# Attention feeding a soft mixture of experts: spread weight loads as halves, move some transposes and the logits in the order of work

## The chip, the cores and the metric

One Trainium2 chip, one of its cores. The metric is the device time of one execution in microseconds (us), the median over several runs. The engines go by these names: PE or TensorE (matrix products and transposes), DVE or VectorE, ACT or ScalarE, POOL or GpSimd, and SP or SyncE, which here only issues transfers (DMAs). A name with q (SPq) is an engine's instruction queue. PSUM is the memory that TensorE writes to.

## The reference, cut to what matters

```python
# 1. attention: 4 batches, 8 heads, 512 local and 32 global positions, head size 64
out_l = softmax(q_l @ [k_g, k_l masked to a window of 32 each side]) @ [v_g, v_l]
out_g = softmax(q_g @ [k_g, k_l]) @ [v_g, v_l]
x = concat(out_g, out_l)                 # as 2176 rows of 512
# 2. soft mixture of experts: 8 experts, 4 slots each
logits = x @ phi                         # phi: 512 x 32
slot_input = softmax(logits over rows).T @ x
slot_out[e] = relu(slot_input[e] @ w1[e]) @ w2[e]   # w1: 512 x 1024, w2: 1024 x 512
x = softmax(logits over slots) @ slot_out
# 3. two dense layers with a squared relu
h = x @ w_in;  out = (relu(h) ** 2) @ w_out
```

## The kernel before

The work has three stages. The attention stage takes the heads in groups of four: eight groups g, two to a batch, and each group in four tiles of 128 rows, so 32 steps n = 4g + uu. The expert stage multiplies the 32 slot inputs with the experts' weights, 32 blocks of 1 MB. The last stage does the two dense layers.

In the attention stage a step has three parts, on different engines. `emit_S` (L357): scores on TensorE (L369) into two PSUM buffers of the pool "S", their minimum on VectorE (L376, the sign is turned), the exponential on ScalarE (L380). `emit_T` (L383): four transposes of the probabilities (L388) into a buffer "T", copied out by ScalarE (L163, the line of the helper `copy_on`). `emit_PV` (L392): products with v (L400), then the division on VectorE (L407 to L409) into `xb`, the tile's output. For each group there are also the global rows: `glob_S` (scores L423 into a buffer "S" and the single buffer "M", minimum L428 to L430, exponentials L434 and L438), `glob_T` and `glob_PV` (L459, copied to `x_g` by four small copies, L471). The pools: "S" has three buffers, "T" three, "M" one, and the products with v one, "X".

When both groups of a batch are through, its four output tiles are transposed (`x_T`, L478: transposes L481, then a copy by ScalarE). Tiles 0 and 3 use a buffer "S" for that, tiles 1 and 2 a buffer "T". `logits` (L486) multiplies the transposed tiles with phi (L493, into "M" in the first three batches), takes the maximum on VectorE (L499), the exponential on ScalarE (L506), and updates running sums (L521, L525). `slot_E` and `slots` (L534, L542) follow. The last batch's work is cut up differently, at the stage's end, but its tiles 0 and 1 go by the same places.

Loads: q and k of two heads come by `load_qk` (L232) on SP into one pair of buffers, and VectorE sorts them (`sort_qk`, L242) before they are transposed (L310, L327); so the next load waits for the sort. v comes by `load_v` (L247): the global part on SP, the local part on POOL from group 2 on. POOL also makes shifted copies of v (`prep_win`, L340), which wait until the products with the old copies are done; VectorE makes others (L350, L352). The expert blocks come on SP into a ring of 13 buffers "w", then into buffers that the attention stage gives up: `more_weights` (L133) issues the next block, `release(n)` raises the limit by n and issues them.

The order of the work is written out by hand: all five engines keep program order (`manual_schedule` with 'PADSG'). `at(when, fn, ...)` gives each piece a place counted in steps, and the pieces are issued in the order of their places. `POS` (L50) holds the places of what occurs once a group, relative to 4g; `LASTPOS` (L51) has other places for the last groups (for group 6 the global scores, transposes and products). The pieces around the change, for a batch whose second group is g, counted from 4g: products of tile 1 at 1.6, x0 at 1.756, global scores at 1.806, scores of the next group's tile 0 at 2.1, transposes of tile 3's probabilities at 2.2, x1 at 2.555; products of tile 2 at 2.6 and tile 3 at 3.6, global products at 3.655, x2 at 3.8, scores at 4.1, x3 at 4.158; scores at 5.1, transposes of probabilities at 5.2, the next q at 5.3, the logits at 5.351, the next k at 5.4. `WAT` (L62) lists the 13 steps at which an expert block is issued, `RELEASE` (L53) the places of the further ones.

Of the kernel before, what the change touches and what calls it, by code (L numbers as in the profile page):

```python
# [9 lines left out]
F32 = mybir.dt.float32  # L10
# [36 lines left out]
MAN = 'PAD'  # L47
MANA = 'PADSG'
ESORT = [0, 0]
POS = {'load0': -7.545, 'sort0': -5.099, 'sort1': -3.55, 'glob_S': 1.806, 'glob_T': 2.7, 'glob_PV': 3.655, 'w1': -2.548, 'w4': -0.34, 'w7': -0.339, 'w10': -1.245, 'w13': 1.7, 'v0': -1.648, 'v1': 0.25, 'x0': 1.756, 'x1': 2.555, 'x2': 3.8, 'x3': 4.158, 'L': 5.351, 'E': 5.8, 'sl': 6.752, 'qg': 1.158}  # L50
LASTPOS = {('glob_S', 6): 0.55, ('glob_T', 6): 1.75, ('glob_PV', 6): 3.35, ('glob_S', 7): -0.3, ('glob_T', 7): 0.35, ('glob_PV', 7): 1.7, ('v0', 7): 0.05, ('v1', 7): 2.05, ('w1', 1): -0.75, ('v0', 0): -0.75, ('sort0', 1): -5.95}  # L51
QGF = 0
RELEASE = ((25.85, 3), (27.75, 1), (29.15, 1), (30.85, 2))  # L53
# [5 lines left out]
EX = 'act'  # L59
EE = 'act'  # L60
EW = 'act'
WAT = [2, 3, 5, 7, 9, 10, 13, 14, 15, 15, 18, 19, 19]  # L62
RECTS = 'A0-1 B0-2 C0-4 A2-6 B3-8 C5-10 A7-12 B9-15 A13-15 C11-15'
RING = 13
MORE = 5
# [8 lines left out]
def kernel(  # L74
# [7 lines left out]
    nc = tc.nc  # L82
    const = ctx.enter_context(tc.tile_pool(name="const", bufs=1))
    ring = ctx.enter_context(tc.tile_pool(name="ring", bufs=RING, side="right"))
# [19 lines left out]
    specs = []  # L104
    for kind, q in UNITS:
        es = slice(2 * q, 2 * q + 2)
        for m in range(4):
            src = (
                w1[es, m * 128:(m + 1) * 128, :].rearrange("e p f -> p e f") if kind == "w1" else
                w2[es, m * 256:(m + 1) * 256, :].rearrange("e (p t) d -> p e (t d)", t=2)  # L110
            )
# [4 lines left out]
    wt, raw = {}, {}  # L116
    w_in32, w_out32 = w_in.bitcast(I32), w_out.bitcast(I32)
    st = {"next": 0, "limit": RING}

    def slot(tag, shape, dt, nm):  # L120
        return ring.tile(shape, dt, tag=tag, name=nm, bufs={"w": RING, "k": MORE, "m": LAST}[tag])

    def load_raw(f, tag="k", halves=(0, 1)):
        if 0 in halves:
            raw[f] = slot(tag, [128, 2048], I32, "raw")
            nc.sync.dma_start(
                out=raw[f][:, 0:1024].rearrange("p (k w) -> p k w", k=4),
                in_=w_in32[:, 256 * f:256 * f + 256].rearrange("(k p) w -> p k w", p=128),
            )
        if 1 in halves:  # L130
            nc.sync.dma_start(out=raw[f][:, 1024:2048], in_=w_out32[128 * f:128 * f + 128, :])

    def more_weights(n=1):  # L133
        for _ in range(n):
            i = st["next"]
            if i >= len(specs) or i >= st["limit"]:
                return
            key, src = specs[i]
            if i == ALL:

                wt[key] = bp.tile([128, NT * 128], F32, tag="cT", name="extra")[:, 0:2048].rearrange(
                    "p (e f) -> p e f", e=2
                )
                nc.sync.dma_start(out=wt[key], in_=src)
                st["next"] += 1
                continue
            j = (i - (i > ALL)) % ALL
            if key[0] == "raw":
                load_raw(0, "w", [key[1]])
                st["next"] += 1  # L150
                continue
            t = slot("w" if j < RING else "k" if j < RING + MORE else "m", list(src.shape), F32, f"ring{i}")
            nc.sync.dma_start(out=t, in_=src)
            wt[key] = t
            st["next"] += 1

    def release(n):
        st["limit"] += n
        more_weights(n)
# [518 lines left out]
    def at(when, fn, *args):  # L678
        order.append((when, len(order), fn, args))
# [7 lines left out]
    for g in range(NG):  # L687
        b, gq = g // 2, g % 2
        a = lambda name: 4 * g + (LASTPOS.get((name, g)) or POS[name])
        for p in range(2):  # L690
# [28 lines left out]
    at(-0.98, load_phi)  # L719
    at(POS["qg"], prep_global_q)  # L720
    at(2.19, slot_sums)
    at(steps - 2 + 0.8, lambda: x_T(B - 1, "g", x_g))
    at(steps - 1 + 0.5, last_xT, B - 1)
    for when in WAT:
        at(when + 0.9, more_weights)
    for when, n in RELEASE:
        at(when, release, n)
    for when, n in BUSYS:
# [8 lines left out]
    x3 = xb[(last, 3)]  # L737
# [154 lines left out]
    t = slot("m", [128, 4, 512], I32, "sgvm")  # L892
# [127 lines left out]
    t = slot("m", [128, 4, 512], I32, "sgvm2")  # L1020
# [169 lines left out]
    for n in range(len(seq)):  # L1190
        credit = min(credit + RATE, 1.2)
        if pieces and n >= START and min(free) <= n:
            kind, f, a, fs = pieces[0]
            if n >= due[kind, f] or (credit >= 1 and not ntile[max(n - 1, -1)]):
                d = 2
# [4 lines left out]
                d = min(d, late)  # L1200
# [59 lines left out]
```

## Time and profile before

| what | value |
|---|---|
| runs | 432.5, 434.31, 431.55 us |
| median of them | 432.5 us |
| profiled execution | 436.24 us |
| its span, first to last instruction | 434.3 us |
| outside the span | 1.9 us |
| mean granted TensorE clock in it, of 1 | 0.981 |

The profiled execution is one more execution, with the profiler on. Its span is what every row of the trace is counted from. In the rows, "[0.69 <-PE sg L423]" at a line's end means that the engine was idle for 0.69 us before the instruction, and that this ended with TensorE's instruction of line 423 that wrote the tile sg. "issue" instead of an engine means that it waited for nothing that the profile shows.

### The profile page before, as it was taken

The numbers are of one execution on the slowest core, as the hardware profiler recorded it, in microseconds if no ns is written. First come the engines' busy times: TensorE is split into PE (matmuls) and PEld (weight loads), VectorE is DVE, ScalarE is ACT, GpSimd is POOL, SyncE is SP. The second block draws the span as 40 slices with busy tenths as digits, with TensorE's granted clock in tenths as the row PEclk, the third lists the DMA queues.
The fourth block names the chain that finished last, engine by engine and source line by source line (L and its number), as shares of the span: only waits on it lengthen the run. The fifth ranks groups of instructions, "written<-read, shape, count | busy, mean of one in ns | idle before, by whom it ended". The sixth has DMA issues, their size and how long they took to land.

```text
span 434.3 us, 11765 instructions
## 1 busy us (share of the span) xinstructions
PE 397.0 (91%) x4530; PEld 289.9 (67%) x4530; DVE 306.9 (71%) x928; ACT 291.7 (67%) x692; POOL 69.2 (16%) x169
## 2 busy tenths in 40 slices
PE   6968888887889889999889999999999999999995
PEld 5747565564566654335667777878788787888883
DVE  2878779775987852436989996897788686735523
ACT  3556777693778761114888898878689786866670
POOL 7326346261743201000000000000000000000000
PEclk9988999996999999999999999999999999999998
DMA  7667696786878698999622232314020000003303
GB/s 184 148 197 208 213 296 204 261 223 236 200 225 258 217 361 339 394 407 375 230 98 97 78 117 54 140 26 169 0 97 2 0 1 2 0 2 145 138 9 121
DMA packets 46247, 70.29 MB, mean 162 GB/s; under 512 B 16336, under 2 KB 32720, under 8 KB 46192
## 3 DMA queue, kind: packets, MB, share of 16 engines
q1 hardware_dynamic: 44560, 66.40, 45.2%
q0 software_dynamic: 1632, 3.15, 3.1%
q8 instruction: 36, 0.59, 0.5%
q14 instruction: 19, 0.16, 0.1%
HBM read 65.08 MB, written 4.46 MB: 160 GB/s over the span
## 4 chain that ended last, share of the span: by engine, by line
PE 69%; DVE 11%; ACT 8%; DMA 5%; issue 4%; SPq 1%; POOL 0%; DVEq 0%; ACTq 0%; POOLq 0%
PE ops L1063 14%; PE ops L1064 14%; PE ops L1065 14%; PE hps L1028 4%; DMA qk<-in_k_l_dram 4%; PE hp L841 3%; PE so L869 3%; PE X L400 2%; PE s L369 2%; DVE tbuf L352 2%; ACT pbuf L380 2%; PE pT L388 2%; DVE pbuf L376 2%; DVE qk L242 1%; DMA v<-in_v_g_dram 1%
## 5 line engine op out<-in xcount | busy, mean ns | idle before, releaser
L1063 PE MATMUL ops<-hl,gh 128*128 128x512 f32 x266 | 105.8, 398 | 0.1
L1064 PE MATMUL ops<-hl,gh 128*128 128x512 f32 x266 | 105.5, 397 | 0.0
L1065 PE MATMUL ops<-hl,gl 128*128 128x512 f32 x266 | 105.0, 395 | 0.4 <-DVE gl L1052 0.4
L1052 DVE TENSOR_TENSOR gl<-r,gh 128x384 fp32r<-128x384 f32 x96 | 50.0, 531 | 28.1 <-ACT r L1047 27.9
L380 ACT ACTIVATE pbuf<-pbuf,nm 128x128 f32<-128x128 f32 x128 | 40.9, 390 | 34.1 <-DVE nm L376 33.7
L1035 ACT ACTIVATE r<-hps 128x384 f32<-128x384 f32 x96 | 45.1, 470 | 24.6 <-PE hps L1028 23.2
L1065 PEld LDWEIGHTS ops<-hl,gl 128*128 128x128 f32 x266 | 50.1, 188 | 13.2 <-DVE gl L1052 0.9
L1063 PEld LDWEIGHTS ops<-hl,gh 128*128 128x128 f32 x266 | 49.9, 188 | 12.1 <-ACT oacc L1075 0.7
L1064 PEld LDWEIGHTS ops<-hl,gh 128*128 128x128 f32 x266 | 50.0, 188 | 8.0
L1047 ACT ACTIVATE r<-r 128x384 f32<-128x384 f32 x96 | 48.7, 507 | 3.0
L1043 ACT ACTIVATE gh<-r 128x384 fp32r<-128x384 f32 x96 | 48.6, 506 | 2.6
L1028 PE MATMUL hps<-cT,wst 128*128 128x384 f32 x96 | 33.6, 353 | 2.1 <-ACT r L1035 2.0
L376 DVE CUSTOM_DVE_ANT_0 pbuf<-s,tbuf 128x128 f32<-128x128 f32 x128 | 29.4, 286 | 8.3 <-PE s L369 7.1
L1079 DVE SCALAR_TENSOR_TENSOR oacc<-ops,oacc 128x512 f32<-128x512 f32 x38 | 24.7, 686 | 4.1 <-PE ops L1065 4.0
L921 DVE SCALAR_TENSOR_TENSOR sgvm<-raw,sgvm 128x512 int32<-128x512 int32 x32 | 22.0, 686 | 5.3 <-ACT sgvm L915 5.3
L388 PE MATMUL pT<-ident,pbuf 128*128 128x128 f32 x128 | 22.1, 298 | 2.9 <-ACT tbuf L163 2.9
L1028 PEld LDWEIGHTS hps<-cT,wst 128*128 128x128 f32 x96 | 17.9, 188 | 9.5 <-ACT r L1035 2.7
L257 POOL DMA_DIRECT2D v<-in_v_l_dram x36 | 23.7, 665 | 0.0
L915 ACT ACTIVATE sgvm<-sgvm,ebias 128x512 int32<-128x512 int32 x32 | 22.8, 712 | 0.5 <-DVE sgvm L909 0.3
L918 DVE SCALAR_TENSOR_TENSOR sgvm<-raw,sgvm 128x512 f32<-128x512 uint32 x32 | 22.0, 686 | 0.1
L388 PEld LDWEIGHTS pT<-ident,pbuf 128*128 128x128 f32 x128 | 14.5, 147 | 9.1 <-ACT tbuf L163 3.9
L976 DVE TENSOR_TENSOR wst<-wpr,misc 128x256 fp32r<-128x256 f32 (+1 forms) x10 | 3.7, 372 | 18.3 <-ACT misc L971 18.3
(201 smaller groups left out, 710.2 us busy)
## 6 DMA issues: line engine op xcount, KB each, us to landing
ring<-in_moe_w_dram SPq DMA_DIRECT2D x31, 1024.0 KB, 8.6
raw<-in_moe_w_in_dram SPq DMA_DIRECT2D x16, 512.0 KB, 4.2
raw<-in_moe_w_out_dram SPq DMA_DIRECT2D x16, 512.0 KB, 5.0
out_dram<-oacc SPq DMA_DIRECT2D x16, 256.0 KB, 2.1
qk<-in_q_l_dram SPq DMA_DIRECT2D x15, 256.0 KB, 3.5
qk<-in_k_l_dram SPq DMA_DIRECT2D x15, 256.0 KB, 4.4
v<-in_v_l_dram POOLq DMA_DIRECT2D x30, 96.0 KB, 4.7
v<-in_v_g_dram SPq DMA_DIRECT2D x48, 32.0 KB, 3.9
```

What stands on the lines that cost most here:

```text
L376: nc.vector.tensor_tensor_reduce(out=dst, in0=ps[h % 2][:, h // 2, :], in1=mask[:, uu, :], scale=1.0, scalar=FAR, op0=ALU.add, op1=ALU.min ...
L380: nc.scalar.activation(out=dst, in_=dst, func=AF.Exp, bias=nm[:, h:h + 1], scale=-1.0)
L388: nc.tensor.transpose(ps[:, 128 * h:128 * h + 128], pt[:, h, :], ident)
L1028: nc.tensor.matmul(ps, wst[:, f, :], cT[:, t0:t0 + n], start=True, stop=True)
L1035: nc.scalar.activation(out=r, in_=ps, func=AF.Relu)
L1043: nc.scalar.activation(out=gh, in_=r, func=AF.Square)
L1047: nc.scalar.activation(out=r, in_=r, func=AF.Square)
L1052: eng.tensor_tensor(out=gL, in0=sq, in1=gh.bitcast(F32), op=ALU.subtract)
L1063: nc.tensor.matmul(ob[tt], gh[:, s], hi, start=first, stop=False)
L1064: nc.tensor.matmul(ob[tt], gh[:, s], lo, start=False, stop=False)
L1065: nc.tensor.matmul(ob[tt], gL[:, s], hi, start=False, stop=last)
L1079: nc.vector.scalar_tensor_tensor(out=t, in0=ps, scalar=WS, in1=t, op0=ALU.mult, op1=ALU.add)
```

## The change

Three places in `POS` change: x0 from 1.756 to 2.25, x2 from 3.8 to 3.25, L from 5.351 to 5.12. The list `WAT` goes; in its place `PACE` has places at which one or two halves of a block are issued by the new `ring_halves`. A half is the part of one of the block's two experts, with a DMA of its own. Where the third entry is True, POOL first writes one element of the half's place in the buffer (a memset), and as the DMA writes there too, SP's issue waits for POOL to have come to this point of its own program. There are five rounds, one for each group from 1 to 5, of one free half, two paced ones, and two (rounds 1 and 2) or one (rounds 3 to 5) paced ones, then two free and two paced ones at 24.9 and 25.71: 26 halves, 19 of them paced, for the same 13 blocks. The places of `RELEASE` stay.

```diff
--- before.py
+++ after.py
@@ -47,7 +47,7 @@
 MAN = 'PAD'
 MANA = 'PADSG'
 ESORT = [0, 0]
-POS = {'load0': -7.545, 'sort0': -5.099, 'sort1': -3.55, 'glob_S': 1.806, 'glob_T': 2.7, 'glob_PV': 3.655, 'w1': -2.548, 'w4': -0.34, 'w7': -0.339, 'w10': -1.245, 'w13': 1.7, 'v0': -1.648, 'v1': 0.25, 'x0': 1.756, 'x1': 2.555, 'x2': 3.8, 'x3': 4.158, 'L': 5.351, 'E': 5.8, 'sl': 6.752, 'qg': 1.158}
+POS = {'load0': -7.545, 'sort0': -5.099, 'sort1': -3.55, 'glob_S': 1.806, 'glob_T': 2.7, 'glob_PV': 3.655, 'w1': -2.548, 'w4': -0.34, 'w7': -0.339, 'w10': -1.245, 'w13': 1.7, 'v0': -1.648, 'v1': 0.25, 'x0': 2.25, 'x1': 2.555, 'x2': 3.25, 'x3': 4.158, 'L': 5.12, 'E': 5.8, 'sl': 6.752, 'qg': 1.158}
 LASTPOS = {('glob_S', 6): 0.55, ('glob_T', 6): 1.75, ('glob_PV', 6): 3.35, ('glob_S', 7): -0.3, ('glob_T', 7): 0.35, ('glob_PV', 7): 1.7, ('v0', 7): 0.05, ('v1', 7): 2.05, ('w1', 1): -0.75, ('v0', 0): -0.75, ('sort0', 1): -5.95}
 QGF = 0
 RELEASE = ((25.85, 3), (27.75, 1), (29.15, 1), (30.85, 2))
@@ -59,7 +59,8 @@
 EX = 'act'
 EE = 'act'
 EW = 'act'
-WAT = [2, 3, 5, 7, 9, 10, 13, 14, 15, 15, 18, 19, 19]
+PACE = [(4 * k + d, n, w) for k in range(1, 6) for d, n, w in ((0.9, 1, False), (1.71, 2, True), (2.76, 2 if k < 3 else 1, True))]
+PACE += [(24.9, 2, False), (25.71, 2, True)]
 RECTS = 'A0-1 B0-2 C0-4 A2-6 B3-8 C5-10 A7-12 B9-15 A13-15 C11-15'
 RING = 13
 MORE = 5
@@ -153,6 +154,24 @@
             nc.sync.dma_start(out=t, in_=src)
             wt[key] = t
             st["next"] += 1
+
+    part = {}
+
+    def ring_halves(n, paced):
+
+        for _ in range(n):
+            key, src = specs[st["next"]]
+            c = part.get("c", 0)
+            if c == 0:
+                part["t"] = slot("w", list(src.shape), F32, f"ring{st['next']}")
+            t = part["t"]
+            if paced:
+                nc.gpsimd.memset(t[0:1, c, 0:1], 0.0)
+            nc.sync.dma_start(out=t[:, c:c + 1], in_=src[:, c:c + 1])
+            part["c"] = 1 - c
+            if c:
+                wt[key] = t
+                st["next"] += 1
 
     def release(n):
         st["limit"] += n
@@ -721,8 +740,8 @@
     at(2.19, slot_sums)
     at(steps - 2 + 0.8, lambda: x_T(B - 1, "g", x_g))
     at(steps - 1 + 0.5, last_xT, B - 1)
-    for when in WAT:
-        at(when + 0.9, more_weights)
+    for when, n, paced in PACE:
+        at(when, ring_halves, n, paced)
     for when, n in RELEASE:
         at(when, release, n)
     for when, n in BUSYS:
```

## Rows read from the trace of the kernel before

**Rows 1.** The page: busy time of the engines; kinds of DMA queue.

```profile
PE 397.0 (91%) x4530; PEld 289.9 (67%) x4530; DVE 306.9 (71%) x928; ACT 291.7 (67%) x692; POOL 69.2 (16%) x169
...
q8 instruction: 36, 0.59, 0.5%
```

**Rows 2.** Stretches: us; busy us (count) of PE, PEld, DVE, ACT, POOL; PEclk; DMA; GB/s.

```profile
92.00:100.00 8.00, 5.66 (x149) 3.69 (x137) 5.53 (x26) 6.40 (x21) 2.65 (x7) 1.00 0.96 298
100.00:108.00 8.00, 7.31 (x117) 4.27 (x118) 3.88 (x16) 2.64 (x9) 0.89 (x2) 0.57 0.57 209
...
116.00:124.00 8.00, 7.06 (x170) 4.93 (x168) 6.26 (x31) 6.64 (x20) 2.33 (x6) 1.00 1.00 316
...
166.00:200.00 34.00, 33.80 (x280) 11.80 (x280) 12.59 (x55) 6.41 (x10) 1.52 (x2) 1.00 0.98 376
```

**Rows 3.** Time line of PE, third batch: start, duration, what, idle before.

```profile
117.72 0.65 PE L481 MATMUL xTp<-ident,xb 128*128 128x128 f32 x4
...
120.52 0.64 PE L369 MATMUL s<-keys,q 64*32 64x128 f32 x24 [0.87 <-ACT xT L163]
```

**Rows 4.** Time line of VectorE, first three batches.

```profile
46.03 0.29 DVE L376 CUSTOM_DVE_ANT_0 pbuf<-s,tbuf 128x128 f32<-128x128 f32 x1 [0.82 <-PE s L369]
...
53.95 0.29 DVE L376 CUSTOM_DVE_ANT_0 pbuf<-s,tbuf 128x128 f32<-128x128 f32 x1 [0.91 <-PE s L369]
...
81.97 0.29 DVE L376 CUSTOM_DVE_ANT_0 pbuf<-s,tbuf 128x128 f32<-128x128 f32 x1 [1.16 <-ACT gbuf L438]
...
119.39 0.66 DVE L428 TENSOR_REDUCE gm<-sg 128x1 f32<-128x480 f32 x1 [0.69 <-PE sg L423]
...
121.18 0.29 DVE L376 CUSTOM_DVE_ANT_0 pbuf<-s,tbuf 128x128 f32<-128x128 f32 x1 [0.81 <-PE s L369]
```

**Rows 5.** Time line of PE: scores of five steps.

```profile
56.26 0.74 PE L369 MATMUL s<-keys,q 64*32 64x128 f32 x32
...
67.26 0.67 PE L369 MATMUL s<-keys,pbuf 64*32 64x128 f32 x32
...
92.27 0.67 PE L369 MATMUL s<-keys,q 64*32 64x128 f32 x32
...
100.69 1.11 PE L369 MATMUL s<-keys,pbuf 64*32 64x128 f32 x32 [2.19 <-issue]
...
107.10 0.67 PE L369 MATMUL s<-keys,pbuf 64*32 64x128 f32 x32
```

**Rows 6.** Time lines of SP and VectorE; a DMA view of 115.6 to 117.

```profile
50.66 0.37 SPq L235 DMA_DIRECT2D qk<-in_q_l_dram  x1
...
116.23 0.98 SPq L235 DMA_DIRECT2D qk<-in_k_l_dram  x1
...
57.69 0.96 DVE L242 COPY qk<-qk 128x512 f32<-128x512 f32 x2
...
126.17 0.59 DVE L242 COPY qk<-qk 128x512 f32<-128x512 f32 x1 [0.26 <-DMA qk<-in_k_l_dram]
...
qk<-in_k_l_dram SPq DMA_DIRECT2D x1, 256.0 KB, 9.9
```

**Rows 7.** Time line of ScalarE, third batch.

```profile
120.47 0.66 ACT L434 ACTIVATE gbuf<-sg,gm 128x480 f32<-128x480 f32 x1
...
126.99 1.28 ACT L380 ACTIVATE pbuf<-pbuf,nm 128x128 f32<-128x128 f32 x4 [2.88 <-DVE nm L376]
```

**Rows 8.** Time line of VectorE, second batch's logits.

```profile
97.28 0.15 DVE L521 COPY nm_run<-nmx 128x1 f32<-128x1 f32 x1 [1.23 <-ACT al L511]
```

**Rows 9.** Time line of PE, third batch's logits.

```profile
134.99 1.08 PE L493 MATMUL L<-xT,phi 128*32 128x128 f32 x32 [0.36 <-ACT gbuf L438]
```

**Rows 10.** Time lines of SP and POOL, end of the attention stage.

```profile
133.77 24.62 SPq L153 DMA_DIRECT2D ring<-in_moe_w_dram  x9
...
137.32 0.40 POOL L343 COPY v<-v 64x260 f32<-64x260 f32 x1 [3.37 <-PE X L400]
...
161.38 0.10 POOL L788 MEMSET ebias<- 128x1 f32 x1 [9.26 <-PE LF L588]
```

## The prediction, made before the change was run

> **What bounds the kernel now.** I read the page first: TensorE is busy 91% of the span, the other engines less [rows 1]. A mean over the span says little, so the table by stretches came next [rows 2]. From 166 to 200 us TensorE is busy 33.8 of 34.0 us while the DMA share is 0.98: the expert stage is TensorE's, with the transfers close behind. After 226 us nothing that the change touches is left. Everything it moves lies in the attention stage, 0 to 166 us, and there no engine is full all the time: work passes round between VectorE, ScalarE and TensorE, and what counts is which wait ends last. So the third view is the time line of each engine, with the idle time ahead of each instruction and what ended it.
>
> In that view three places repeat. In each of the first three batches TensorE does the first tile's output transposes (L481), then the global scores (L423), then scores L369; it stops inside L369, 0.87 us in the third batch, until ScalarE has copied those transposes out [rows 3]. They hold one of the three buffers "S", and L369 needs it. VectorE stands idle twice for this: 0.69 us ahead of the global minimum L428 (the same 0.69 in all three batches) and 0.82, 1.16 and 0.81 us ahead of the scores' minimum L376 [rows 4]. For the middle one the profile names ScalarE's L438 as what ended it; I count it with the others, since the same stop stands ahead of it.
>
> The second place is the stretch behind 92 us. [...] From the step at 92.27 to the one at 107.10 us are 14.8 us; the same two steps of the batch before (56.26 to 67.26) took 11.0 [rows 5].
>
> The third is what looks like the largest entry and is not. The chain of waits puts a k_l load, issued at 116.23 us behind two expert blocks, at 9.9 us, but VectorE lost 0.26 us to it: it had other work until 125.9 [rows 6].
>
> **The change part by part.** The sum is made against the profiled execution's 436.24 us, whose span is 434.3.
>
> *x0 behind the probabilities' transposes (three batches).* It removes 0.6 us of transposes ahead of the global scores and the stop for ScalarE inside L369. VectorE's two idles, 1.51, 1.85 and 1.50 us by batch [rows 4], become about 0.1 each: the global scores begin where the transposes began, 0.6 us sooner, and L369 follows without a stop. What is late next: the moved transposes take the buffer of the global scores and wait for ScalarE's exponential of them. In the third batch that one begins at 120.47 [rows 7]; it loses 0.6 us of queue ahead of it, so TensorE would stop near 120 for some 0.5 us instead of 0.87. In the second and third batch VectorE then has work without a break for 5 us (its next idle is at 126.17) and ScalarE has 2.88 us idle ahead of its own next step [rows 6, 7], so the gain should hold: 1.5 and 1.4. In the first batch VectorE waits again at 53.95 us for TensorE's scores, 0.91 us [rows 4], so there TensorE is the limit and only its own 0.87 minus 0.5 counts: 0.5 with rounding up. Sum 3.4; ends 0 (every gain met by the new stop) and 4.9. I stand nearer the upper end because the waits named are direct. In the last batch x0 only changes places with one probabilities' transpose while TensorE waits for other things: 0.
>
> *x2 from behind the global outputs to behind the probabilities' transposes.* Four transposes, 0.6 us on TensorE, the same on both sides; on ScalarE its copy (0.60 us) changes places with four small copies of the global outputs. The copies are queued behind the same exponentials, so nothing leaves ScalarE's busy stretch: 0, ends -0.5 and +0.5 a batch (the length of the copy), I take 0.
>
> *Logits ahead of the transposes.* In the first two batches VectorE's idle at the logits (1.23 us ahead of L521 in the second [rows 8]) shortens, since ScalarE does the exponential ahead of two copies; but ScalarE is full there and has the same list before the keys on which the next global scores wait. So the order inside a full stretch changes: gain 0.2 each, ends 0 and 1.2. In the third batch the global scores come earlier (place 24.55), and the logits share the single buffer "M" with them: already now L493 at 134.99 waits for ScalarE's L438 [rows 9]. Put ahead, it holds up the probabilities' transposes and the next group's q, which now use the time before it: two groups of four at some 0.6 us each, so about 1.1 us of TensorE work falls behind the wait. TensorE does have idle time later in this batch, so I take a loss of 0.7, ends 0 and 1.4. Together +0.3.
>
> *Halves and pacing.* 13 loads become 26, of which 19 follow a memset on POOL. One small memset takes 0.10 us [rows 10]: 1.9 us in all, in front of which POOL waits anyway (3.37 us in the one shown), so 0; without that cover it would be 1.9. Thirteen more issues on SP, of about the 0.37 us of the q load in rows 6, beside its long waits: 0; without them 4.8. [...]
> The new wait is SP's: a paced half waits until POOL has reached it. Behind it in SP's queue are the loads of q and k for the next pair of heads, v_g, and at the end the released blocks. The pair at 6.76 and its like stands right ahead of a q/k load that waits for VectorE's sort anyway, and POOL gets there first, so the q/k load itself is not held, but up to 1 MB moves with it. The last pair (25.71) waits for POOL's copy that begins at 137.32 us, while the first released block is now issued at 133.77 [rows 10]: three blocks leave 4.4 us later, with one of the ring still ahead of them. That one and the nine that now go out from 133.77 to 158.4 are ten blocks, 10.5 MB; at the 376 GB/s of 166 to 200 us [rows 2] they take 27.9 us from 138.2, until 166.1. The expert stage begins at 166 with blocks that landed long before, and takes these ten last: hidden. If it weren't, TensorE would wait for blocks in a stage where it is full, up to those 4.4 us.
> The gain: the 0.26 us of the sort, taken as 0.3, and the trough behind 92 us. Its 14.8 - 11.0 = 3.8 us began behind a stretch, 92 to 100 us, in which the DMA share was 0.96 [rows 2]: SP issues three whole blocks there between a v and a q/k load. By the new places half a block goes out there, and a whole one some steps later. I take the halt to be the instruction stream of TensorE being late behind that traffic (the profile's page has a queue for instructions, 36 packets [rows 1]), and let the 3.8 go. Ends 0 and 3.8.
> [...]
>
> **Sum.** 436.24 - 3.4 (x0) + 0.3 (logits) - 3.8 (trough) - 0.3 (sort) + 0.1 (landings) = 429.1. The median of the runs is 432.5, 3.7 below the profiled one, about the size of the trough. I take it that the other runs were mostly without it, so that against the median 3.3 us, 0.8%, are left: 429.1 us.
>
> **The rivals.**
> *The waits only change places.* The new stop of x0 behind the global exponential and the logits' wait for "M" cost what the old stop did. For it: all three engines are busy 6 to 7 us of 8 in 116 to 124 us [rows 2]. Against it: 2.88 us of ScalarE idle right behind [rows 7]. The x0 term is then 0 to 0.8: 432.5.
> *Everything counts.* All 4.9 us of VectorE's idle go, and the logits give 1.2 in two batches: 432.5 - 4.9 - 2.4 = 425.2. Against it: the first batch is TensorE's at 53.95.
> *The halt is not from load traffic.* Then 436.24 - 3.4 + 0.3 - 0.3 + 0.1 = 432.9 wherever the trough comes up. [...]
> *Slower: pacing makes q and k late.* A q/k load behind two whole blocks took 9.9 us to land, and VectorE was only just covered [rows 6]. In an early group the sort comes 7.0 us after the issue (50.66 to 57.69 [rows 6]). If the half or whole megabyte issued just ahead makes the load take 8.5 us, each of the five groups loses 1.5 us, 7.5 in all, on top of the forecast's 429.1: 436.6, and 438 with one such load at the full 9.9. It decides from a landing of some 7 us on. Against it: a whole block in flight beside a q/k load is the present state too, and the paced halves leave before the q/k load.
>
> **How the numbers follow.** Forecast 0.45 (427 to 431); places changed 0.22; everything counts 0.20; halt not from traffic 0.05; slower 0.08. About 1% (4.3 us) is what a measurement of this kernel can tell from no change. Under 428.2 lie the third case whole and two fifths of the forecast: 0.38. Over 436.8 lies the slower case and a little of the far ends of others: 0.10. Between: 0.52. For eight in ten I leave out the slower case and the far ends of the others: 424.5 to 433.5.
>
> **What would show it.** Right: no idle ahead of L428 and L376 at the three places, no stop inside L369 for ScalarE, x0's transposes behind the probabilities' with a short stop; no stretch of lower clock between 90 and 110 us; q/k landings of at most 7 us; the expert stage as long as before. Wrong: VectorE idle ahead of its sorts, TensorE waiting for blocks after the attention stage, or as much idle on VectorE as now behind new releasers.

## The result, and the profile after

The changed kernel took 435.86 us (median of 8 runs, 433.97 to 439.69); the kernel before, beside it, 432.69 us (8 runs, 429.50 to 437.18). The ratio is 1.0067, 95% interval 1.0039 to 1.0096: slower by 0.7%, about 3.2 us. The forecast was 429.1 us, faster by 0.8%, with a range up to 433.5. It was wrong in size and in sign.

The profiled execution of the changed kernel took 436.44 us (span 434.4), that of before 436.24 us (span 434.3): the one of before was among its longer ones. The two traces are therefore compared place by place, and times by their ratios.

The totals say little: TensorE is as busy as before. The instruction queue moved the same 36 packets [rows 1].

```profile
PE 395.0 (91%) x4530; PEld 291.4 (67%) x4530; DVE 306.5 (71%) x928; ACT 292.0 (67%) x692; POOL 70.2 (16%) x188
...
q8 instruction: 36, 0.59, 0.6%
```

VectorE's time line shows what x0 brought. The idle of 0.69 us ahead of the global minimum (L428 of before, now L447) is gone. The idle ahead of the scores' minimum (L376, now L395) is not: 0.76, 0.99 and 0.76 us, where it was 0.82, 1.16 and 0.81 [rows 4].

```profile
42.47 0.66 DVE L447 TENSOR_REDUCE gm<-sg 128x1 f32<-128x480 f32 x1
44.21 0.29 DVE L395 CUSTOM_DVE_ANT_0 pbuf<-s,tbuf 128x128 f32<-128x128 f32 x1 [0.76 <-ACT gbuf L453]
...
81.59 0.29 DVE L395 CUSTOM_DVE_ANT_0 pbuf<-s,tbuf 128x128 f32<-128x128 f32 x1 [0.99 <-ACT gbuf L457]
...
113.92 0.66 DVE L447 TENSOR_REDUCE gm<-sg 128x1 f32<-128x480 f32 x1
115.66 0.29 DVE L395 CUSTOM_DVE_ANT_0 pbuf<-s,tbuf 128x128 f32<-128x128 f32 x1 [0.76 <-ACT gbuf L453]
...
134.19 0.16 DVE L426 TENSOR_SCALAR rc<-X 128x4 f32<-128x4 f32 x1 [1.69 <-PE X L419]
```

One wait is new: the sort of q and k in an early group, which waited for nothing before (57.69 in [rows 6]), now waits for both loads. They were issued at 49.24 and 49.71 us, right behind a round's halves, and took 6.3 and 7.1 us to land.

```profile
55.65 0.43 DVE L261 COPY qk<-qk 128x512 f32<-128x512 f32 x1 [0.53 <-DMA qk<-in_q_l_dram]
56.92 0.43 DVE L261 COPY qk<-qk 128x512 f32<-128x512 f32 x1 [0.84 <-DMA qk<-in_k_l_dram]
```

TensorE's time line says why the stop stayed, and where time went. In the third batch L388 (L369 of before) still stops, as long as before (0.88 against 0.87 us [rows 3]), but for another copy of ScalarE, that of the keys. The third batch's logits at 129.31 wait 2.34 us for ScalarE's exponential of the global scores (0.36 before [rows 9]), and behind them VectorE waits 1.69 us for X (its last row above). Three rows begin behind idle time that nothing in the profile explains, "issue"; the last two lie at the end of the attention stage, where before had nothing of the kind.

```profile
57.75 0.42 PE L388 MATMUL s<-keys,q 64*32 64x128 f32 x8 [3.31 <-issue]
...
115.06 0.45 PE L388 MATMUL s<-keys,q 64*32 64x128 f32 x16 [0.88 <-ACT keys L182]
...
129.31 1.43 PE L512 MATMUL L<-xT,phi 128*32 128x128 f32 x32 [2.34 <-ACT gbuf L457]
...
143.43 0.45 PE L388 MATMUL s<-keys,pbuf 64*32 64x128 f32 x15 [0.76 <-issue]
...
150.00 0.22 PE L419 MATMUL X<-v,tbuf 128*32 128x65 f32 x1 [2.19 <-issue]
```

The queues show what stands around those last two. SP issues four halves, the last pair among them, and reaches their end only at 135.97; POOL frees the pair with two memsets at 135.05. The nine released blocks begin at 136.08 (133.77 before [rows 10]).

```profile
125.23 10.74 SPq L170 DMA_DIRECT2D ring<-in_moe_w_dram  x4
136.08 21.90 SPq L154 DMA_DIRECT2D ring<-in_moe_w_dram  x9
```
```profile
135.05 0.12 POOL L169 MEMSET ring<- 1x1 f32 x2
```

The stretches (columns as in [rows 2]) show no trough behind 92 us: the clock is 1.00 over 100 to 108. Later, SP's wait leaves the DMA engines at 0.48 over 132 to 140, then everything goes at once: share 1.02 and 404 GB/s over 140 to 148, where TensorE works only 6.12 of 8 us, and the granted clock is 0.83 in the stretch after it: right behind the second halt it falls, to 0.50 over 151 to 153, and from 154 on it is 1.00 again. The kernel before, in the second fence, had 0.82 in both stretches. From 166 us on TensorE is full, as in [rows 2].

```profile
92.00:100.00 8.00, 6.84 (x192) 4.91 (x191) 6.10 (x33) 6.28 (x20) 2.16 (x8) 1.00 0.72 214
100.00:108.00 8.00, 6.79 (x174) 4.79 (x174) 7.65 (x34) 4.67 (x17) 4.98 (x11) 1.00 0.68 228
...
132.00:140.00 8.00, 8.00 (x227) 5.68 (x229) 5.17 (x28) 5.32 (x18) 1.72 (x6) 0.92 0.48 166
140.00:148.00 8.00, 6.12 (x182) 3.93 (x173) 6.70 (x31) 5.74 (x18) 1.96 (x6) 1.00 1.02 404
148.00:158.00 10.00, 7.64 (x167) 6.31 (x166) 4.46 (x16) 5.10 (x13) 0.67 (x2) 0.83 0.90 346
...
166.00:200.00 34.00, 33.75 (x284) 11.92 (x286) 12.39 (x55) 6.53 (x11) 1.52 (x2) 1.00 0.96 362
```

```profile
132.00:140.00 8.00, 7.64 (x231) 5.71 (x227) 6.06 (x30) 6.83 (x23) 1.81 (x5) 1.00 0.82 248
140.00:148.00 8.00, 7.12 (x197) 4.04 (x188) 6.53 (x30) 5.55 (x16) 2.65 (x7) 1.00 0.82 314
```

And the chain of waits (start, length, what) has the second halt on it:

```profile
147.81 2.19 issue
```

One comparison sums it up. The attention stage's last scores minimum (the first row before, the second after) begins 3.4 us sooner. From there to the end of the span it is 287.6 us after and 284.1 before: what the profiled execution of after had gained by then, it lost again, 3.1 us of it before the expert stage's first product (18.8 us behind that minimum against 15.7).

```profile
150.22 0.28 DVE L376 CUSTOM_DVE_ANT_0 pbuf<-s,tbuf 128x128 f32<-128x128 f32 x1
...
146.83 0.28 DVE L395 CUSTOM_DVE_ANT_0 pbuf<-s,tbuf 128x128 f32<-128x128 f32 x1
```

### The profile page after: what moved, and what is told of

The parts are those of the page before. It is cut to its first block, busy times and chain, and to the rows that moved or that the text cites. A ratio compares the mean times of both kernels' runs of the same rounds, so it can differ in the third digit from the quotient of the medians.

```text
span 434.4 us, 11813 instructions
## 1 busy us (share of the span) xinstructions
PE 395.0 (91%) x4530; PEld 291.4 (67%) x4530; DVE 306.5 (71%) x928; ACT 292.0 (67%) x692; POOL 70.2 (16%) x188
## 4 chain that ended last, share of the span: by engine, by line
PE 71%; DVE 13%; ACT 5%; issue 5%; DMA 4%; SPq 0%; POOL 0%; DVEq 0%; ACTq 0%; POOLq 0%
PE ops L1082 14%; PE ops L1083 14%; PE ops L1084 14%; PE hps L1047 4%; PE hp L860 3%; PE so L888 3%; PE s L388 2%; DVE pbuf L395 2%; DMA ring<-in_moe_w_dram 2%; PE pT L407 2%; PE X L419 2%; DVE qk L261 1%; DVE tbuf L371 1%; PE busy L653 1%; PE xTp L500 1%
## 5 line engine op out<-in xcount | busy, mean ns | idle before, releaser
L395 DVE CUSTOM_DVE_ANT_0 pbuf<-s,tbuf 128x128 f32<-128x128 f32 x128 | 29.5, 285 | 4.4 <-PE s L388 1.7
L388 PE MATMUL s<-keys,q 64*32 64x128 f32 x512 | 13.3, 276 | 7.4 <-issue 4.1
```

What stands on the lines that cost most here:

```text
L395: nc.vector.tensor_tensor_reduce(out=dst, in0=ps[h % 2][:, h // 2, :], in1=mask[:, uu, :], scale=1.0, scalar=FAR, op0=ALU.add, op1=ALU.min ...
```

## The experiments

In the edits, `PACE` lists (place, number of halves, paced or not), and the letters of the theories are those of the expectations. "Halt" is idle time of TensorE that its time line gives to "issue".

**The loads alone** (new loads, old places of x0, x2 and L), **the places alone** (whole blocks at their old times, new places), **the changed kernel with its last pair free**, and **with the logits put back.**

```diff
--- after, e1: the old places
-'x0': 2.25, 'x1': 2.555, 'x2': 3.25, 'x3': 4.158, 'L': 5.12,
+'x0': 1.756, 'x1': 2.555, 'x2': 3.8, 'x3': 4.158, 'L': 5.351,
--- before, e2: the new places
-'x0': 1.756, 'x1': 2.555, 'x2': 3.8, 'x3': 4.158, 'L': 5.351,
+'x0': 2.25, 'x1': 2.555, 'x2': 3.25, 'x3': 4.158, 'L': 5.12,
--- after, e3
-PACE += [(24.9, 2, False), (25.71, 2, True)]
+PACE += [(24.9, 2, False), (25.71, 2, False)]
--- after, e4
-'L': 5.12,
+'L': 5.351,
```

> Only the loads change (halves, pacing); x0, x2 and the logits stay at their old places. Theory A (the new spread of the loads makes the blocks of TensorE's instructions late, and holds up the released blocks at the end): 436 to 437.5 us, slower than before by 3 to 5, with several halts of TensorE put down to 'issue', 8 us or more together. Theory B (the new places cost: the logits wait for buffer M, x0's transposes wait for the global exponential): 432 to 433.5, as before. Theory C (each part alone is harmless, only both together cost): 431.5 to 433.

> Only x0, x2 and the logits change places; the loads stay 13 whole blocks. Theory A: 429.5 to 431.5 us, faster than before by 1 to 3, since VectorE's waits at the global scores go. Theory B: 435.5 to 436.5, as the changed kernel, with the logits' wait for M in the third batch 2 us or more. Theory C: 431 to 433.

> The changed kernel with the last pair of halves (25.71) not paced, so that the released blocks behind it on SP are not held by POOL. Theory A, for its part at the end of the attention stage: 434 to 435 us, 1 to 2 less than the changed kernel's 435.9, the DMA share of 140 to 148 us falls from 1.02 and the halt of 2.2 us at 147.8 goes. Theory B: no difference, 435.5 to 436.5.

> The changed kernel with the logits alone back at 5.351. Theory A: no difference to the changed kernel beyond 0.5 us, 435.4 to 436.4. Theory B: 433 to 434.5, since the third batch's wait for M (2.3 us of TensorE) shrinks to the 0.4 us of before.

Measured: loads alone 1.0065 (1.0026 to 1.0103), places alone 0.9997 (0.9953 to 1.0041), last pair free 0.9999 (0.9963 to 1.0036), logits back 1.0023 (0.9987 to 1.0059). The loads alone are as slow as the whole change, and freeing one pair of halves brings it back level with before; so far Theory A. But the places alone, which it had 1 to 3 us faster, are level too, and with the logits put back the median, 433.88 us, is in Theory B's range (its interval overlaps that of the changed kernel). So the loads lose, and something in the places takes back what the places gain. TensorE's time line of the loads alone, and of the logits put back, has the two late halts of the changed kernel; that of the places alone and of the last pair free has none behind 105 us.

```profile
140.58 0.59 PE L388 MATMUL s<-keys,pbuf 64*32 64x128 f32 x18 [0.74 <-issue]
...
147.24 0.24 PE L419 MATMUL X<-tbuf 128*32 128x65 f32 x1 [2.18 <-issue]
```

With the last pair free, SP gets to the released blocks at 124.24, 11.8 us sooner, and the full stretch no longer falls on 140 to 148 (time line of SP, then stretches). The DMA engines are full over 124 to 132 instead, where the granted clock is 0.57, and again over 148 to 158; neither brings a halt:

```profile
121.17 2.95 SPq L170 DMA_DIRECT2D ring<-in_moe_w_dram  x4
124.24 28.00 SPq L154 DMA_DIRECT2D ring<-in_moe_w_dram  x9
```
```profile
124.00:132.00 8.00, 6.48 (x82) 5.50 (x83) 3.45 (x22) 4.70 (x15) 0.65 (x2) 0.57 1.03 348
132.00:140.00 8.00, 7.25 (x228) 4.10 (x226) 5.95 (x29) 5.33 (x17) 2.80 (x8) 1.00 0.91 348
140.00:148.00 8.00, 7.20 (x187) 5.61 (x187) 7.48 (x34) 6.10 (x19) 0.80 (x2) 1.00 0.60 233
148.00:158.00 10.00, 8.31 (x139) 6.19 (x139) 4.37 (x18) 5.31 (x16) 0.10 (x1) 1.00 1.02 394
```

With the logits put back, the third batch's wait is 1.12 us instead of 2.34, and the interval from the scores' minimum ahead of them to the next is 5.0 us (127.83 to 132.82) instead of 6.7 (128.94 to 135.62). But the late halts are still there:

```profile
128.20 1.08 PE L512 MATMUL L<-xT,phi 128*32 128x128 f32 x32 [1.12 <-ACT gbuf L457]
...
140.07 0.45 PE L388 MATMUL s<-keys,pbuf 64*32 64x128 f32 x16 [0.91 <-issue]
146.54 0.22 PE L419 MATMUL X<-v,tbuf 128*32 128x65 f32 x1 [2.14 <-issue]
```

**Is it the hold or the halves?** The kernel before, whole blocks and old places, with only its last two loads ahead of the release moved to the change's times and the second of them held behind POOL (e5); the loads alone with the last pair free (e6); the changed kernel with the last pair free and only the third batch's logits put back (e7); the places alone with the same logits put back (e8).

```diff
--- before, e5
-WAT = [2, 3, 5, 7, 9, 10, 13, 14, 15, 15, 18, 19, 19]
+WAT = [2, 3, 5, 7, 9, 10, 13, 14, 15, 15, 18]
...
+            if paced:
+                nc.gpsimd.memset(t[0:1, 0, 0:1], 0.0)
...
+    at(24.9, more_weights)
+    at(25.71, more_weights, 1, True)
--- e1, e6: the last pair free
-(25.71, 2, True)
+(25.71, 2, False)
--- e3, e7; and e2, e8
-('sort0', 1): -5.95}
+('sort0', 1): -5.95, ('L', 5): 5.351}
```

> The kernel before, whole blocks and old places, with its last two blocks of the ring at 24.9 (free) and 25.71 (behind a memset on POOL, as in the changed kernel), so that the released blocks behind it on SP are held. Theory D (what costs is the held queue: some four blocks then go out at once at 136 to 148 us, and two blocks of TensorE's instructions come late behind them): ratio to before 1.005 to 1.008, halts of TensorE of about 1.0 and 2.4 us between 138 and 152 us, DMA share 1.0 from 140 to 148. Theory E (the halves themselves cost): ratio 0.998 to 1.002 and no such halts.

> Halves and pacing at the old places of x0, x2 and the logits, only the last pair not paced. Theory D: ratio to before 0.997 to 1.001, no halts between 138 and 152 us. Theory E: 1.004 to 1.007, as with the last pair paced.

> The changed kernel with the last pair not paced and the third batch's logits alone back at 5.351. If the parts add up as the steps of the traces show (x0 0.65 us in each of three batches, the logits 0.3 and 0.15 in the first two, nothing lost in the third): 2.4 us less than before, ratio 0.993 to 0.997. Rival (the gains are taken back by new halts, as VectorE's and TensorE's lead is used up at the next late block of instructions): 0.998 to 1.001.

> Whole blocks as before; x0, x2 and the logits at their new places but for the third batch's logits at 5.351. Adding up: ratio 0.993 to 0.997. Rival: 0.998 to 1.001. The step from the third batch's scores of the tile ahead of the logits to those behind falls from 6.7 us back to 5.0 in either case.

Measured: e5 1.0070 (1.0037 to 1.0102), e6 1.0039 (1.0006 to 1.0072), e7 1.0006 (0.9967 to 1.0044), e8 0.9938 (0.9903 to 0.9974).

e5 bears Theory D out: before, which has no late halt of its own, gets both of them, and the whole loss, without any halves. But e5 also moves its last two blocks from place 19.9 to 24.9 and 25.71, and no kernel has whole blocks there with none held; so it doesn't tell the hold from the late place. Its time lines of POOL, SP and TensorE:

```profile
133.83 0.09 POOL L154 MEMSET ring<- 1x1 f32 x1
```
```profile
125.00 31.41 SPq L155 DMA_DIRECT2D ring<-in_moe_w_dram  x11
```
```profile
142.02 0.59 PE L371 MATMUL s<-keys,pbuf 64*32 64x128 f32 x18 [0.63 <-issue]
...
148.92 0.24 PE L402 MATMUL X<-tbuf 128*32 128x65 f32 x1 [2.25 <-issue]
```

e8 is faster than both kernels. Its logits wait 0.94 us, its intervals are those of before there, and its only halt behind 130 us is 0.17:

```profile
127.32 0.95 PE L493 MATMUL L<-xT,phi 128*32 128x128 f32 x25 [0.94 <-ACT gbuf L438]
...
138.45 0.45 PE L369 MATMUL s<-keys,pbuf 64*32 64x128 f32 x16 [0.17 <-issue]
```

e6 and e7 are misses. With the last pair free, halts of the same size came all the same, a few microseconds sooner (e6, then e7), and e7 gained nothing over e3 by its logits:

```profile
138.28 0.44 PE L388 MATMUL s<-keys,pbuf 64*32 64x128 f32 x12 [1.61 <-issue]
...
144.25 0.59 PE L388 MATMUL s<-keys,pbuf 64*32 64x128 f32 x18 [1.58 <-issue]
```
```profile
133.38 0.43 PE L388 MATMUL s<-keys,pbuf 64*32 64x128 f32 x10 [0.73 <-issue]
139.41 0.45 PE L388 MATMUL s<-keys,pbuf 64*32 64x128 f32 x16 [1.67 <-issue]
```

So with the last pair held the halts are there each time (four kernels of four: after, e1, e4, e5); freeing it takes them away in e3 and not in e6 and e7. The hold alone does not explain them, and the last four kernels ask what does.

**Fill the ring early, with and without pacing.** All halves of the last pair go out in the rounds before, so that nothing stands ahead of the released blocks (e9); the same with the third batch's logits back (e10); that with no half paced (e11); and the changed kernel as it is with no half paced (e12).

```diff
--- after, e9, e10 and e11 (the last two with the logits of e7)
-(0.9, 1, False), (1.71, 2, True), (2.76, 2 if k < 3 else 1, True))]
-PACE += [(24.9, 2, False), (25.71, 2, True)]
+(0.9, 1, False), (1.71, 2, True), (2.76, 2, True))]
+PACE += [(22.77, 1, False)]
--- e11 and e12, besides
-        at(when, ring_halves, n, paced)
+        at(when, ring_halves, n, False)
```

> The changed kernel, its places and its pacing, but the last four halves go out in rounds 3 to 5 and at 22.77, so that the ring is full before the released blocks. Theory F (the cost is the last two megabytes of the ring right ahead of the released blocks, whose traffic makes two blocks of TensorE's instructions late in a row, whether paced or not): ratio to before 0.997 to 1.001, against 1.0067 for the changed kernel, and no halts over 1 us between 131 and 152 us. Theory E (halves cost wherever they stand): 1.003 to 1.007.

> The same with the third batch's logits back at 5.351. Theory F: 0.992 to 0.996, as whole blocks with these places (0.9938), no halts over 1 us between 131 and 152 us. Theory E: 0.998 to 1.002, as the halves with the last pair free and these places (1.0006).

> The same as the run before with no half paced: the memsets on POOL and SP's waits for them are left out. If the pacing itself is worth or costs nothing: within 0.003 of the run before. Rival (pacing keeps the traffic apart and saves halts): 0.003 to 0.008 slower than the run before, with halts of over 1 us back between 40 and 110 us.

> The changed kernel with every half issued freely: no memset on POOL ahead of any half; blocks as halves, times of the halves, and the new places of x0, x2 and L as changed. It lies between the kernel with only the last pair free (ratio 0.9999) and the one with early halves, nothing paced and the third batch's logits back (0.9950). Theory D alone (only the held last pair costs): the same as with the last pair free, 0.998 to 1.002, 432 to 433.5 us. Theory G (pacing inside the rounds costs too, since it sends the halves out right ahead of q, k and v loads): 0.994 to 0.998, some 430 to 431.5 us, and the q and k loads of the later groups land sooner than in the changed kernel. Theory H (free halves bring the trough of the second batch back, which pacing was to avoid): 1.003 or more, with a halt of over 1.5 us of TensorE between 90 and 110 us.

Measured: e9 1.0025 (0.9990 to 1.0059), e10 1.0055 (1.0024 to 1.0087), e11 0.9950 (0.9914 to 0.9986), e12 0.9956 (0.9923 to 0.9989). No row of e9 is shown; its ratio lies above Theory F's range, and its interval reaches into it.

e10 has no halt behind 100 us, and is slow all the same: Theory F was right on the halts and wrong on the time. What e10 shows is the "slower" rival of the prediction. The last half of a paced round waits for POOL, leaves at 120.2 us right ahead of the last group's q and k, and they and the v behind them come late (time lines of SP, VectorE and POOL):

```profile
112.01 8.19 SPq L170 DMA_DIRECT2D ring<-in_moe_w_dram  x6
120.33 0.38 SPq L254 DMA_DIRECT2D qk<-in_q_l_dram  x1
```
```profile
127.75 0.43 DVE L261 COPY qk<-qk 128x512 f32<-128x512 f32 x1 [1.31 <-DMA qk<-in_q_l_dram]
```
```profile
129.75 0.40 POOL L362 COPY tbuf<-v 64x260 f32<-64x260 f32 x1 [3.12 <-DMA v<-in_v_l_dram]
```

In e11, the same but free, the same six halves are issued within 4.28 us, four and more ahead of the next q and k, and neither wait is there:

```profile
110.91 4.28 SPq L170 DMA_DIRECT2D ring<-in_moe_w_dram  x6
```

Behind those late loads the granted clock of e10 is 0.66 over 132 to 140, against 1.00 in e11, so that part of e10's loss is the clock's. e10 to e11 is 1.0% for the pacing alone, which neither side of e11's expectation had, and e12 against the changed kernel 1.1%. e3 lies between them at 0.9999: of those 1.1%, the last pair is 0.7 and the rounds 0.4, as Theory G had it. The landings that it named are sooner in two early groups (q and k take 3.9 and 4.1 us in e12 where the changed kernel has 6.3 and 7.1, then 3.4 and 3.7 against 5.6 and 5.1), and VectorE's two waits there are gone; in the later groups the two kernels differ by at most 1.3 us. H has fallen: free halves brought no trough (no halt over 0.8 us between 90 and 110 us in e12). The intervals of e3 and e12 overlap, so the share of the rounds is less sure than the other. Nor do halves themselves cost anything that shows: e11, all halves and none paced, stands at 0.9950, e8, whole blocks with the same places, at 0.9938. Theory E has fallen.

e12 also tells what e6 and e7 left open. It holds nothing, and it has a late halt too, of 1.53 us at 139.94. What the kernels with late halts share is a full DMA queue about that time (e12's stretch here, all kernels in the table below):

```profile
132.00:140.00 8.00, 6.10 (x197) 3.23 (x194) 6.02 (x28) 5.29 (x16) 2.64 (x7) 1.00 1.01 393
```

## Why the prediction was wrong

The prediction's sum, beside what the steps measured. An interval is the time from one scores' minimum to the next on VectorE, taken where no halt lay in it in either kernel.

- **x0: 3.4 us forecast (0.5, 1.5 and 1.4 by batch), about 1.95 measured.** The intervals that hold it went from 4.31, 4.67 and 4.32 us to 3.67, 4.02 and 3.68, 0.65 each. This is the idle of 0.69 ahead of the global minimum and nothing else. The step that failed is "L369 follows without a stop". ScalarE's copies of keys and of the transposes end within 0.5 us of each other (119.98 and 120.46 in the third batch of before, below); I named the last of the two as what held L369. With that gone the global scores begin 0.6 us sooner behind the products ahead of them, the copy of the keys ends no sooner, and the stop of 0.88 us stands behind it. The price that I gave for the moved transposes' own stop hardly came up.

```profile
119.33 0.65 ACT L163 ACTIVATE keys<-tk 128x480 f32<-128x480 f32 x2
119.86 0.60 ACT L163 ACTIVATE xT<-xTp 128x512 f32<-128x512 f32 x1
```

- **x2: 0 forecast**; no interval shows anything else.
- **Logits: +0.3 forecast, about +1.8 measured.** In the first two batches the sign and size were right: the intervals are 4.88 and 5.06 us in e2 against 5.20 and 5.21 in e1, a gain of 0.47 together (0.4 forecast). In the third batch the loss was taken as 0.7 with ends 0 and 1.4; it is 2.3: 6.68 against 5.00 us in the interval of the logits, 3.02 against 2.40 in the next. The mechanism was the one named (L waits for the buffer "M", and what it held up falls behind the wait), but I counted only TensorE's own work behind it. VectorE needs that work: it then waits 1.69 us for X.
- **The trough: 3.8 us forecast against the profiled execution, 0 against the median.** The halt of 2.19 us that it began with [rows 5] is not in the trace of after, and neither is a stretch at a clock of 0.57 behind it, but that is not shown to be the new loads' doing: with the old loads e8 has no halt over 0.4 us between 90 and 110, e2 one of 0.48 and e5 one of 0.83, and the clock is 1.00 over 100 to 108 in all three. That the median of before stands for executions without it was an assumption; the sum below is in line with it. Halts of its kind stand elsewhere in every trace: 0.66, 3.31, 1.19 and 0.79 us between 50 and 93 in after.
- **The sort and the landings: -0.3 and +0.1.** VectorE's wait of 0.26 us is gone, and waits of 0.53 and 0.84 us stand ahead of an earlier sort (55.65 and 56.92), which the prediction had named as a sign of being wrong. No run shows the 0.1 for landings: TensorE's trace has 160 semaphore instructions before and 156 after.
- **POOL's memsets and SP's issues: 0 forecast**, and 0.12 us for two on POOL.
- **The last pair: hidden forecast, 3.5 us measured.** This is the step that turned the sign. The prediction had SP held to 138.2 us (136.0 measured) and the ten blocks behind it on the wire until 166, and asked only whether the expert stage would wait for those blocks. It does not. What suffers is the attention stage's own end, while they pass: TensorE stands there for 0.76 and 2.19 us that the profile puts to "issue". For the trough the prediction had taken such a halt to be instructions late behind traffic, and it did not ask for one here.

By kernel: from the last scores' minimum to the end of the span, idle "issue" time of TensorE behind 130 us, and the DMA share over 132 to 140 and 140 to 148. Each row's times are of one execution, and executions of one kernel lie 4 to 9 us apart.

```
kernel                        ratio    last minimum   to the end   halts (us)         DMA share
before                        1        150.22         284.1        0                  0.82 0.82
after                         1.0067   146.83         287.6        0.76 + 2.19        0.48 1.02
e1 loads alone                1.0065   144.09         287.5        0.74 + 2.18        0.82 1.02
e4 logits back                1.0023   143.42         288.6        0.91 + 2.14        0.91 1.03
e5 whole block held           1.0070   145.66         288.3        1.41 + 0.63 + 2.25 0.64 1.02
e2 places alone               0.9997   143.59         284.2        0                  0.84 0.62
e3 last pair free             0.9999   144.16         283.9        0                  0.91 0.60
e8 places, third logits back  0.9938   142.53         284.3        0.17               0.85 0.61
e11 early, free, same logits  0.9950   143.85         283.9        0                  0.86 0.61
e6 loads alone, pair free     1.0039   147.51         284.0        1.61 + 1.58        1.03 0.64
e7 pair free, logits back     1.0006   142.52         285.8        0.73 + 1.67        1.03 0.79
e12 nothing paced             0.9956   143.04         285.3        1.53               1.01 0.62
e10 early, paced, logits back 1.0055   149.12         285.8        0                  0.78 0.53
```

The four with the pair held need 287.5 to 288.6 us, the five without a halt before 166 that counts (before, e2, e3, e8, e11) 283.9 to 284.3: a loss of some 3.5 us, of which the second halt is 2.2. Most of the rest is time at a lower granted clock: right behind the halt in after and e1 (0.83 over 148 to 158), and in the expert stage in e4 (0.83 over 158 to 168) and e5 (0.72 over 164 to 170). From the expert stage's first product to the dense layers' first it is 42.3 and 42.4 us in those two, 40.4 to 40.7 in the kernels whose clock stays at 1.00 there. That part is not the hold's alone: e7, e12 and e10, with nothing held at the end, have 42.0 to 42.2 (clock 0.79 over 158 to 166 in e7 and e12, 0.72 over 164 to 170 in e10), which is why they need 1.0 to 1.9 us more than the five. In e6, e7 and e12 the halts come sooner, all of them ahead of the last minimum. e10 loses the rest of its time ahead of it too. The stretch of e12:

```profile
158.00:166.00 8.00, 7.46 (x49) 2.17 (x51) 1.17 (x7) 1.00 (x3) 1.22 (x1) 0.79 0.59 230
```

The last column parts the kernels cleanly. All seven with a halt over 0.4 us behind 130 have a share of 1.01 or more in one of the two stretches; the six without have at most 0.91 in both. The split was seen after the runs, and none was made to test it. By it the hold does not make the halts by itself. It moves the full stretch to 140 to 148, and the second halt with it to behind the last minimum, where nothing takes it up: the expert stage's first product comes 18.1 to 18.8 us behind that minimum in the four, 15.7 in the five. In e3 the full stretch came sooner, over 124 to 132, at a granted clock of 0.57, and brought none; whether it does so in e3's other executions, one trace can't say.

Summed: -1.95 (x0) - 0.47 + 2.3 (logits) + 3.5 (held pair) = +3.4 us; the runs say +3.2. The same terms give +1.5 for e4 (1.0035; measured 1.0023), -2.4 for e8 and e11 (0.9944; 0.9938 and 0.9950), -0.1 for e2 and e3 (0.9998; 0.9997 and 0.9999) and +3.5 for e1 and e5 (1.0081; 1.0065 and 1.0070). They miss e10 (0.9944 against 1.0055), whose late loads are shown above, e6 (1.0000 against 1.0039) and e7 (0.9944 against 1.0006), whose halts the sum has no term for, and e12 (0.9998 against 0.9956). The first three have the rounds paced and are slower than the sum; e12 has not and is faster. e9 (0.9998) measured 1.0025, and its interval holds the sum. The terms were read from these same traces, so that the agreement is a check of them and not a forecast. The pacing of the rounds has a price, but of its size the sum says nothing: e3 has it and fits without a term for it. Why e12 gains beyond the sum, with a late halt of its own, stays open.

Of the rivals, "the waits only change places" had 0 to 0.8 for x0, so that the 1.95 lies between it and the forecast. The "slower" one had a right culprit, pacing, and mostly the wrong place: it put the price on five groups' q and k loads, while after shows waits in one group (1.37 us together), and e10 in an early and in its last group.

## What to carry to other kernels

A load that waited in SP's queue held what stood behind it (the nine released blocks began at 136.08 us, and at 124.24 with the pair free): price not only who needs those loads, but what else is on the wire when they all leave together, and on what work that full stretch falls. To pace transfers by another engine is to choose a moment that one doesn't see; here sending the halves at once was worth 1.1% against it. And where a stop is to be taken away, list the other things that the stopped instruction waits for, with the times at which they end: the gain was only up to the next of them, 0.65 us of the 1.5 to 1.85 of VectorE's idle by batch.

## What the hardware did that I had not expected

The halts have a place. Count TensorE's instructions in the trace from 0 (weight loads, matmuls, semaphores): those of after stand ahead of numbers 1729, 1985, 3265, 3521, 5825 and 6081, those of before ahead of 961, 1473, 2497 and 3777. All are 193 plus a multiple of 256. The 36 packets of the instruction queue hold 16 KB each in both traces, 0.59 MB together; spread over TensorE's 9223 instructions before and 9219 after, that is some 64 bytes for each, and some 256 of them to a packet. The packets and these blocks of 256 are paired here in their order.

Over the twelve executions of the changed and tried kernels that are read here and the one of before, TensorE crosses 308 such places between 20 and 170 us. At 71 of them over 0.4 us lies between the starts of the instruction ahead and the one behind, where any other place of a block has such a gap 2 times on average, and all 57 halts over 0.4 us of these traces and this time stand there. In no case does the block begin sooner than 1.19 us after its packet landed; in half of the 71 it begins within 1.43 us, among the 237 others half begin 2.5 us or more after it. The packet starts 1.6 us (median) after the place before it where nothing halts and 3.6 where something does; 98.2 to 99.4 is the packet ahead of the halt of before at 100.69, and 147.5 to 148.6 that ahead of the one of after at 150.00. The packet also follows the traffic. Where the DMA share from 1 us ahead of the place before to 3 us behind it is under 0.5, the packet starts 0.85 us (median) behind that place, and none of 46 crossings halts; where it is 0.9 or more, the packet starts 2.8 us behind it, and 38 of 100 halt. So the packet starts about when the block before it begins (four of the 308 start ahead of that, by up to 1.8 us), later where there is more traffic, and the halts stand where it starts late. A block lasts some 6 us in the attention stage. In the expert stage, with DMA shares of 0.96 to 1.03, a block lasts 14 to 15 us (156.8 to 170.6 to 185.7 in before), and no halt is over 0.42. That the traffic delays the packet, and that its landing ends the halt, is my reading of this agreement; no run delays a packet alone. Of the 3.5 us that the change lost behind the last minimum, 2.2 were one such halt.
